# Attention and channel mix on one core: weight loads on 128 partitions, 64-row transposes joined with the k-v sums, two batches mixed out of PSUM, a new order

## The chip, the cores and the metric

The kernel runs on one core of a Trainium2 chip. The metric is the device time of one execution in microseconds (us). One core has five engines that run side by side, each with its own queue of instructions in a fixed order: TensorE (PE, matmuls and transposes), VectorE (DVE), ScalarE (ACT), GpSimd (POOL) and SyncE (SP). SP, ACT and POOL also issue DMAs. Matmul results land in PSUM, 8 banks of 2 KB for each of 128 partitions; everything else lives in SBUF.

## The reference

Linear attention feeds a channel mix in the manner of RWKV. With 8 batches, 8 heads, 576 positions, head width 64, 512 channels and 1024 hidden channels:

```python
q_s = softmax(q, over the 64 channels);  k_s = softmax(k, over the 576 positions)
kv = einsum('bhsd,bhse->bhde', k_s, v)
x  = einsum('bhsd,bhde->bhse', q_s, kv)          # then (batch, position, head*64 + e)
x_prev = x shifted by one position, zeros ahead
xk = mu_k * x + (1 - mu_k) * x_prev
xr = mu_r * x + (1 - mu_r) * x_prev
k = maximum(xk @ w_k, 0);  v = k * k @ w_v;  r = sigmoid(xr @ w_r)
out = r * v
```

The kernel leaves the subtraction of the maximum out, computes in bf16 with float32 sums, and writes the sigmoid by way of tanh.

## The kernel before, in words

**Attention** works on groups: batch b and g = 0 or 1, four heads each, two of them (u = 0, 1) side by side in 128 channels and two (hf = 0, 1) above each other in partitions 0 to 63 and 64 to 127. A partition holds nine neighbouring positions (j = 0 to 8), which makes each load one run of 9*64 floats per head. For each group ACT takes the exponentials of q and k (L423) and casts v (L430), DVE sums q's exponentials over the channels (L437), inverts (L440) and scales (L445), PE transposes the scaled q, nine times 128x128 (L472), and ACT copies the result out (L476). PE sums k-v in 18 matmuls of 64 rows, the two row halves alternating (L453); a column of ones beside v gives k's sum, whose reciprocal (L460, L464) scales the k-v matrix into a weight (L560). PE's X (L566) is then x, transposed: channels on partitions, positions in the order (position in 9, run).

**Mixing.** With that order the previous position is the column 64 to the left, and the first 64 columns come from the end ("edge"). For batches 1 to 7, ACT copies X out (L571) and DVE does edge (L575), difference (L579), scaling by mu (L584) and addition (L589), into xk and xr. For batch 0 the mixing is done on PE: the k-v matrix is multiplied by masks that hold mu and 1-mu (L513, masks built by POOL on L350 and L351), five matmuls (L525) add both terms in PSUM, and one copy each (L530) brings xk and xr out. xk and xr are rings of four batches.

**Main work** runs in units of 512 columns of the ring (and one of 256 per half): k tiles (L646, four matmuls each) with relu on ACT (L631) and square on DVE (L635); then per 128 columns an r tile (L677) with tanh on ACT (L682), a v tile in two halves (L687), the product on DVE (L693) and two stores issued by SP (L703).

**The order** of every engine is written out ahead by a planner (class Plan). An operation has an engine, a length, a due time (`key`), the operations that it depends on and the buffers that it takes and gives back. Due times of the main work come from a clock that starts at MAIN and goes on by PACE times each length; due times of earlier steps are counted back from those that use them, less a lead (`early`, from AHEAD: 1, 4 and 8 us for batch 0, batch 1 and the rest). The planner then plays the engines forward and takes for each the operation that is ready first, by due time among those ready. Loads are issued by ACT, SP and POOL in the order FIRST for batch 0 and by POOL for the rest, behind the weights, in the order of their keys, of which SOON changes a few. POOL's weights wait for the seventh load of batch 0 (GATE). PSUM has four single banks `mm` for main work and two pairs of banks `att`; batch 0's k-v sums use `mm` (pool "early").

Of the kernel before, what the change touches and what calls it, by code (L numbers as in the profile page):

```python
# [15 lines left out]

START = 0.7
HOP = 0.05
LATE = 1e6
SPARE = 0  # L20
LOOK = {"PE": 0.03, "ACT": 0.2, "DVE": 0.1, "POOL": 0.03, "SP": 0.03}
AHEAD = (1.0, 4, 8)
MAIN = 17.0
PACE = 1.148
DMA_RATE = 365.0
DMA_LEAD = 2.5
DMA_TAIL = 0.6

PARTS = {1: [slice(0, 2)], 2: [slice(0, 1), slice(1, 2)]}
FIRST = ((0, 0, ("ACT", "ACT")), (1, 0, ("SP", "SP")), (0, 1, ("ACT", "SP")),  # L30
         (0, 2, ("SP", "SP")), (1, 1, ("SP", "SP")), (1, 2, ("SP", "SP")))
ORDER = (0, 1, 2)
SOON = {(1, 0, 0): 2.2, (1, 0, 1): 2.4, (1, 1, 0): 2.7, (1, 0, 2): 3.5}
GATE = 6
FILL = 0
ON_PE = (0,)
CASTS = (("ACT", "ACT"), ("ACT", "ACT"))
EVAC = ((("ACT", "DVE"), ("ACT", "ACT")), (("ACT", "DVE"), ("ACT", "ACT")))
# [3 lines left out]

# [7 lines left out]
class Op:  # L50


    def __init__(self, engine, occ, lat, key, emit, deps, takes, gives, size):
        self.engine, self.occ, self.lat, self.key = engine, occ, lat, key
        self.emit, self.deps, self.takes, self.size = emit, list(deps), list(takes), size
        self.start = self.end = None
        self.early = 0.0
        for slot in gives:
            slot.last.append(self)


class Plan:

    def __init__(self, pools, shared):
        self.pools = {name: [shared.get((name, i), [(name, i)]) for i in range(n)]
                      for name, n in pools.items()}  # L70
        self.user = {}
        self.ops = []

    def add(self, engine, occ, lat, key, emit, deps=(), takes=(), gives=(), size=0.0):
        op = Op(engine, occ, lat, key, emit, [d for d in deps if d is not None], takes, gives,
                size)
        self.ops.append(op)
        return op

    def slot_time(self, slot):  # L80
        best = None
        for i, parts in enumerate(self.pools[slot.pool]):
            free = 0.0
            for user in (self.user.get(part) for part in parts):
                if user is not None:
                    late = [o.end for o in user.last]
                    free = None if not late or None in late or free is None else max(
                        [free] + late)
            if free is not None and (best is None or free < best[0]):
                best = (free, i)  # L90
        return best
# [9 lines left out]
    def set_due(self):  # L101
        after = {}
        for op in self.ops:
            for d in op.deps:
                after.setdefault(d, []).append(op)
        seen = set()
        for root in self.ops:
            stack = [(root, False)]
            while stack:
                op, closed = stack.pop()  # L110
                if closed and not op.size:
                    for o in after.get(op, ()):
                        op.key = min(op.key, o.key - op.lat - HOP - SPARE)
                    op.key -= op.early
                elif op not in seen:
                    seen.add(op)
                    stack.append((op, True))
                    stack += [(o, False) for o in after.get(op, ())]

    def order(self):  # L120
        self.set_due()
        free = {}
        self.pe_busy = []
        dma_free = 0.0
        waiting = {}
        for op in self.ops:
            waiting.setdefault(op.engine, []).append(op)
        done = []
        left = len(self.ops)
        while left:  # L130
            chosen = None
            for engine, ops in waiting.items():
                now = free.get(engine, START)
                ready = None
                for op in ops:
                    if any(d.end is None for d in op.deps):
                        continue
                    t = max([now] + [d.end + HOP for d in op.deps])
                    ok = True
                    for slot in op.takes:  # L140
                        got = self.slot_time(slot)
                        if got is None:
                            ok = False
                            break
                        t = max(t, got[0] + HOP)
                    if not ok:
                        continue
                    rank = (max(t, now + LOOK[engine]), op.key)
                    if ready is None or rank < ready[0]:
                        ready = (rank, t, op)  # L150
# [4 lines left out]
            for slot in op.takes:  # L155
                slot.index = self.slot_time(slot)[1]
# [8 lines left out]
            elif op.size:  # L165
                dma_free = max(dma_free, t + DMA_LEAD) + op.size / DMA_RATE
# [4 lines left out]
            waiting[op.engine].remove(op)  # L171
            done.append(op)
            left -= 1
        return sorted(done, key=lambda o: o.start)


@with_exitstack
def kernel(
# [13 lines left out]

    B, H, S, D = q.shape
    C = H * D
    F = moe_w_k.shape[1]
    assert S == 576 and D == 64 and H == 8, f"{q.shape=}"
    J = S // 64
    CT = C // 128
    FT = F // 128
    RING = 4 * S  # L200
    UNITS = ((0, 512), (512, 512), (1024, 512), (1536, 512), (2048, 256))
    assert B % 4 == 0

    pools = {"raw": 12, "eq": 3, "ek": 2, "vv": 2, "stat": 4, "qs": 2, "qt": 3, "w": 3, "wp": 4,
             "rz": 3, "xb": 2, "xd": 2, "xm": 3, "k2": 2, "rel": 3, "th": 2, "ot": 3, "mm": 4,
             "att": 2, "early": 2}
    shared = {("early", i): [("mm", 2 * i), ("mm", 2 * i + 1)] for i in range(2)}
    plan = Plan(pools, shared)
# [5 lines left out]
    def buffers(name, shape, dtype, space=None):  # L214
        return [(space or const).tile(shape, dtype, name=f"{name}_{'abcdefghijklmnop'[i]}")
                for i in range(pools[name])]

    raws = buffers("raw", [128, 2, J * D], F32)
    eqs = buffers("eq", [128, J, 2, D], BF16)
    eks = buffers("ek", [128, J, 2, D], BF16)  # L220
    vvs = buffers("vv", [128, J, 130], BF16)
    rsums = [const.tile([128, 2 * J], F32, name=f"rsum_{x}") for x in "abcd"]
    rrecs = [const.tile([128, 2 * J], F32, name=f"rrec_{x}") for x in "abcd"]
    qss = buffers("qs", [128, J, 128], BF16)
    qts = buffers("qt", [128, J, 128], BF16)
    ws = buffers("w", [128, 2, 128], BF16)
    wps = buffers("wp", [128, 2, 2, 128], BF16)
    rzs = buffers("rz", [128, 2], F32)
    xbs = buffers("xb", [128, 2, 64 + S], BF16)
    xds = buffers("xd", [128, 2, S], BF16)  # L230
    xms = buffers("xm", [128, 2, S], BF16)
    k2s = buffers("k2", [128, FT, 512], BF16)
    rels = buffers("rel", [128, 512], BF16)
# [66 lines left out]
    def emit_identity():  # L300
        make_identity(nc, ident[:])
# [468 lines left out]
```

## Time and profile before

| | us |
|---|---|
| median of three runs | 212.07 |
| lowest, highest | 210.74, 212.23 |
| profiled execution, first to last instruction (its span; its own total is not given) | 210.3 |
| PE busy | 192.2 (91%) |
| DVE busy | 160.3 (76%) |
| ACT busy | 150.9 (72%) |
| POOL busy | 43.2 (21%) |
| mean DMA rate over the span | 193 GB/s |

Slices of the page are a fortieth of the span, and a digit is the busy share in tenths. Rows of the chain give start, length and what ran; rows of the timeline give start, length, engine, line, operation, output and inputs, count, and in brackets the idle time ahead and what ended it. A matmul's own row is longer than its share, since matmuls overlap; the chain shows the share. Times are counted from the span's start.

### The profile page before, as it was taken

What the parts mean: (1) busy time and instruction counts of PE and PEld (TensorE: products, weight loads), DVE (VectorE), ACT (ScalarE), POOL (GpSimd) and SP (SyncE); (2) the same over time, 40 slices, a digit from 0 to 9 for tenths busy, and PEclk for the clock granted to TensorE, in tenths of its full rate; (3) what the DMA queues carried; (4) which work ended last, traced back from release to release, by engine and by line L of the source; (5) the groups of instructions that cost most, each with busy time, mean ns of one, the idle gap of its engine ahead of it and who ended that gap; (6) DMA issues with size and microseconds to landing.
All of it is one profiled execution on the core that took longest, in us unless ns stands there. A gap on an engine that the chain in (4) does not pass through costs nothing.

```text
span 210.3 us, 3597 instructions
## 1 busy us (share of the span) xinstructions
PE 192.2 (91%) x1283; PEld 97.2 (46%) x1283; DVE 160.3 (76%) x364; ACT 150.9 (72%) x229; POOL 43.2 (21%) x72
## 2 busy tenths in 40 slices
PE   3089998967999999999999999999999999999991
PEld 0065444433544544445467444445444554444740
DVE  6488684999999999999959995957796469632531
ACT  5596798998999999759599977338964862452440
POOL 3793656534334132301100000000000000000000
PEclk9999999999999999999999999999999999999999
DMA  6999999999999999983871130350034003502424
GB/s 216 367 215 201 346 267 394 392 405 403 392 395 404 404 383 339 317 277 112 245 196 41 31 69 0 71 119 14 6 86 111 2 3 85 115 0 50 102 51 100
DMA packets 15898, 40.62 MB, mean 193 GB/s; under 512 B 2300, under 2 KB 3848, under 8 KB 15880
## 3 DMA queue, kind: packets, MB, share of 16 engines
q0 software_dynamic: 8384, 27.40, 39.7%
q1 hardware_dynamic: 7064, 12.10, 20.4%
q10 hardware_dynamic: 432, 0.88, 1.3%
q8 instruction: 10, 0.16, 0.3%
q14 instruction: 8, 0.07, 0.1%
HBM read 33.56 MB, written 9.44 MB: 204 GB/s over the span
## 4 chain that ended last, share of the span: by engine, by line
PE 82%; DVE 7%; ACT 4%; DMA 3%; issue 1%; ACTq 0%; DVEq 0%
PE mm_b L646 9%; PE mm_c L646 8%; PE mm_a L687 7%; PE mm_d L687 7%; PE mm_b L687 7%; PE mm_a L646 6%; PE mm_c L687 6%; PE mm_d L677 5%; PE mm_d L646 5%; PE mm_c L677 4%; DMA raw_b<-in_k_dram 3%; PE mm_a L677 2%; PE att_a L472 2%; PE att_a L453 2%; PE att_b L453 2%; PE att_b L472 2%
## 5 line engine op out<-in xcount | busy, mean ns | idle before, releaser
L646 PEld LDWEIGHTS <-wk_bf 128*128 128x128 bf16 x320 | 30.4, 98 | 31.0 <-issue 2.3
L646 PE MATMUL mm_b<-xk,wk_bf 128*128 128x512 bf16 (+1 forms) x96 | 23.2, 357 | 0.0
L646 PE MATMUL mm_c<-xk,wk_bf 128*128 128x512 bf16 (+1 forms) x92 | 22.6, 361 | 0.0
L677 PEld LDWEIGHTS <-xr 128*128 128x128 bf16 x144 | 13.4, 98 | 16.0 <-issue 0.7
L687 PEld LDWEIGHTS <-k_a 128*128 128x128 bf16 x144 | 13.5, 98 | 15.8 <-issue 0.5
L687 PEld LDWEIGHTS <-k_b 128*128 128x128 bf16 x144 | 13.4, 98 | 15.7
L646 PE MATMUL mm_a<-xk,wk_bf 128*128 128x512 bf16 (+1 forms) x72 | 17.1, 355 | 0.0
L646 PE MATMUL mm_d<-xk,wk_bf 128*128 128x512 bf16 (+1 forms) x60 | 14.9, 358 | 1.6 <-DVE xk L589 1.6
L677 PE MATMUL mm_d<-wr_bf,xr 128*128 128x512 bf16 x56 | 14.4, 379 | 0.0
L687 PE MATMUL mm_a<-wv_bf,k_a 128*128 128x512 bf16 x48 | 12.3, 379 | 0.0
L682 ACT ACTIVATE th_a<-mm_d 128x512 f32<-128x512 f32 x12 | 7.2, 602 | 6.8 <-PE mm_d L677 6.6
L677 PE MATMUL mm_c<-wr_bf,xr 128*128 128x512 bf16 x40 | 10.3, 379 | 0.1
L687 PE MATMUL mm_d<-wv_bf,k_a 128*128 128x512 bf16 x40 | 10.3, 379 | 0.0
L687 PE MATMUL mm_c<-wv_bf,k_b 128*128 128x512 bf16 x40 | 10.3, 379 | 0.0
L687 PE MATMUL mm_b<-wv_bf,k_b 128*128 128x512 bf16 x40 | 10.1, 379 | 0.0
L472 PEld LDWEIGHTS <-qs_a 128*128 128x128 bf16 x72 | 4.9, 103 | 8.6 <-DVE qs_a L445 7.4
L635 DVE TENSOR_TENSOR k_a<-rel_a 128x512 bf16<-128x512 bf16 (+1 forms) x13 | 5.1, 391 | 4.6 <-ACT rel_a L631 4.5
L631 ACT ACTIVATE rel_a<-mm_b 128x512 bf16<-128x512 f32 (+1 forms) x10 | 5.4, 539 | 4.0 <-PE mm_b L646 3.8
L687 PE MATMUL mm_a<-wv_bf,k_b 128*128 128x512 bf16 x32 | 8.2, 379 | 0.0
L687 PE MATMUL mm_d<-wv_bf,k_b 128*128 128x512 bf16 x32 | 8.2, 379 | 0.0
L687 PE MATMUL mm_c<-wv_bf,k_a 128*128 128x512 bf16 x32 | 8.2, 379 | 0.0
L682 ACT ACTIVATE th_b<-mm_a 128x512 f32<-128x512 f32 x6 | 3.6, 594 | 6.3 <-PE mm_a L677 6.3
(258 smaller groups left out, 452.5 us busy)
## 6 DMA issues: line engine op xcount, KB each, us to landing
out_dram<-ot_a SPq DMA_DIRECT2D x24, 128.0 KB, 2.7
out_dram<-ot_b SPq DMA_DIRECT2D x24, 128.0 KB, 2.4
out_dram<-ot_c SPq DMA_DIRECT2D x24, 128.0 KB, 2.7
raw_a<-in_q_dram POOLq DMA_DIRECT2D x3, 576.0 KB, 10.3
raw_c<-in_k_dram POOLq DMA_DIRECT2D x2, 576.0 KB, 10.3
raw_b<-in_v_dram POOLq DMA_DIRECT2D x2, 576.0 KB, 10.5
raw_d<-in_q_dram POOLq DMA_DIRECT2D x2, 576.0 KB, 10.2
raw_e<-in_k_dram POOLq DMA_DIRECT2D x2, 576.0 KB, 10.9
```

The source lines that it names most:

```text
L453: nc.tensor.matmul(kv_of(kvp, hf)[:, 0:129], lhsT=eks[ek.index][r, j, :, :].rearrange("p u d -> p (u d)"), rhs=vvs[vv.index][r, j, 0:129], ...
L472: nc.tensor.transpose(out=transposed()[:, j, :], in_=qss[qs.index][:, j, :], identity=ident[:])
L631: nc.scalar.activation(out=rels[rel.index][:, 0:n], in_=bank(kf)[:, 0:n], func=ACT.Relu, scale=HALF_ROOT)
L635: nc.vector.tensor_tensor(out=k2s[k2.index][:, fc, 0:n], in0=rels[rel.index][:, 0:n], in1=rels[rel.index][:, 0:n], op=ALU.mult)
L646: nc.tensor.matmul(bank(kf)[:, 0:n], lhsT=wk_bf[:, ct, fc * 128:(fc + 1) * 128], rhs=xs[0][:, ct, c0:c0 + n], start=(ct == 0), stop=(ct == ...
L677: nc.tensor.matmul(bank(rps), lhsT=xs[1][:, ct, c:c + 128], rhs=wr_bf[:, ct, :], start=(ct == 0), stop=(ct == CT - 1))
L682: nc.scalar.activation(out=ths[th.index][:], in_=bank(rps), func=ACT.Tanh, scale=0.5)
L687: nc.tensor.matmul(bank(vps), lhsT=k2s[k2.index][:, ft, 128 * m:128 * m + 128], rhs=wv_bf[:, ft, :], start=(ft == 0), stop=(ft == FT - 1))
```

## The change

- **Weights.** w_k and w_r were loaded to partitions 0 to 63 and 64 to 127 by two DMAs each; now one DMA writes 128 partitions, with row 2e+u on a partition where it was 64u+e. w_k is split by columns (two tiles of 512) instead of by channel tiles. The k-v weight `w` is written with the same interleaving (last index u), so that X comes out in that order, and mu is turned to it by a copy ahead of its transpose.
- **Transposes.** Nine of 128x128 become 18 of 64 rows by 128 columns, one half into each bank of a pair. For batches 2 to 7 they and the 18 k-v matmuls are one block on PE that takes both `att` buffers; for batches 0 and 1 (SPLIT) they stay separate.
- **Mixing.** Batches 0 and 1 (FUSED): X into PSUM as for the others; for each of xk and xr and each hf, ACT copies X out scaled by 1-mu, DVE copies the edge, and one DVE operation takes mu times X from PSUM plus the shifted copy. Masks, their loads and their operations are gone. Batches 2 to 7 keep the earlier mixing.
- **Order.** New constants; a lead for each batch and group; due times aren't counted back through main operations; three passes, each with main operations due when the last pass started them; FIRST has k of group 0 ahead of q of group 1; of batch 1 to 7 one load (q of batch 2, group 0) goes ahead of w_v and all of batch 1; only units 0 and 1 split their k tiles by channel halves, for their first four tiles; tanh is due earlier.
- **Buffers and tail.** Three instead of two of ek, vv and qs; five output tiles for three. The very last tile's v is computed in two halves of 256 columns, each stored by SP and ACT.

```diff
-AHEAD = (1.0, 4, 8)
-MAIN = 17.0
-PACE = 1.148
+MAIN = 17.837
+PACE = 1.101
-FIRST = ((0, 0, ("ACT", "ACT")), (1, 0, ("SP", "SP")), (0, 1, ("ACT", "SP")),
-         (0, 2, ("SP", "SP")), (1, 1, ("SP", "SP")), (1, 2, ("SP", "SP")))
-SOON = {(1, 0, 0): 2.2, (1, 0, 1): 2.4, (1, 1, 0): 2.7, (1, 0, 2): 3.5}
-ON_PE = (0,)
+FUSED = (0, 1)
+SPLIT = (0, 1)
+EARLY_UNITS = 2
+AHEAD = {(0, 0): 4.01, (0, 1): 1.59, (1, 0): 6.36, (1, 1): 1.67, (2, 0): 13.33, (2, 1): 9.59,
+        (3, 0): 9.47, (3, 1): 9.29, (4, 0): 7.84, (4, 1): 8.09, (5, 0): 3.2, (5, 1): 7.98, (6,
+        0): 2.31, (6, 1): 12.19, (7, 0): 5.85, (7, 1): 5.11}
+FIRST = ((0, 0, ("ACT", "SP")), (0, 1, ("ACT", "SP")), (1, 0, ("SP", "SP")), (0, 2, ("SP",
+        "SP")), (1, 1, ("SP", "SP")), (1, 2, ("ACT", "SP")))
+SOON = {(2, 0, 0): 2.63}
+PASSES = 3
...
-    def weight_part(dst, src, n, u, c0, c1):
-        ap = bass.AP(tensor=src.tensor, offset=src.offset + (4 * u + c0) * D * n,
-                     ap=[[n, 64], [D * n, c1 - c0], [1, n]])
-        return nc.gpsimd.dma_start(out=dst[64 * u:64 * u + 64, c0:c1, :], in_=ap)
+    def weight(dst, src, n, col, width, gated=False):
+        ap = bass.AP(tensor=src.tensor, offset=src.offset + col,
+                     ap=[[n, D], [4 * D * n, 2], [D * n, CT], [1, width]])
+        ld = kn.nc.gpsimd.dma_start(out=dst[:], in_=ap)
...
-    mask_zeros = plan.add("DVE", 1.8, 1.9, 0, emit_mask_zeros)
-    rows_load = plan.add("SP", 0.9, 0.9, -600, emit_mu_rows_load, size=10.0)
-    rows_done = plan.add("PE", 0.86, 0.98, -501, emit_mu_rows, [rows_load, consts], [rows_slot])
-    wide = plan.add("ACT", 0.48, 0.6, 0, emit_mu_wide, [rows_done], [], [rows_slot])
-    mu_masked = [plan.add("POOL", 1.55, 1.6, -2 + m, lambda m=m: emit_mu_mask(m),
-                          [wide, mask_zeros]) for m in range(2)]
+    mu_turn = add("DVE", 0.2, 0.28, LATE, emit_mu_turn, [mu_load])
+    mu_done = add("DVE", 0.16, 0.26, LATE, emit_mu_copy, [mu_t], gives=[mu_slot])
+    mu_done.early = 6.0
...
         def transpose_q():
             for j in range(J):
-                nc.tensor.transpose(out=transposed()[:, j, :], in_=qss[qs.index][:, j, :],
-                                    identity=ident[:])
+                for hf in range(2):
+                    r = slice(64 * hf, 64 * hf + 64)
+                    kn.nc.tensor.transpose(out=turned(hf)[:, j, :],
+                                           in_=kn.qss[qs.index][r, j, :],
+                                           identity=kn.ident[r, r])
...
+        if split:
+            tr = add("PE", 0.5, 0.67, step, transpose_q, scaled + [identity], [qtp], [qs],
+                     name=f"T{tag}")
+            kvm = add("PE", 0.73, 0.8, step, kv, expk + castv, [kvp], [ek, vv], name=f"KV{tag}")
+        else:
+            def block():
+                transpose_q()
+                kv()
+            tr = kvm = add("PE", 1.1, 1.2, step, block, scaled + [identity] + expk + castv,
+                           [qtp, kvp], [qs, ek, vv], name=f"TKV{tag}")
...
+        if b in FUSED:
...
+                    def rest(xe=xe, hf=hf, c=c):
+                        kn.nc.scalar.activation(out=kn.xes[xe.index][:, hf, 64:64 + S],
+                                                in_=flat(xp[hf])[:, 0:S], func=ACT.Copy,
+                                                scale=kn.rest[:, c:c + 1])
+                    def edge(xe=xe, hf=hf):
+                        t = kn.xes[xe.index]
+                        kn.nc.vector.tensor_copy(out=t[:, hf, 1:64], in_=t[:, hf, 576:639])
+                    def fuse(xe=xe, hf=hf, c=c, m=m):
+                        kn.nc.vector.scalar_tensor_tensor(
+                            out=kn.xs[m][:, 2 * g + hf, c0:c0 + S], in0=flat(xp[hf])[:, 0:S],
+                            scalar=kn.mu[:, c:c + 1], in1=kn.xes[xe.index][:, hf, 0:S],
+                            op0=ALU.mult, op1=ALU.add)
...
+            parts = [slice(0, 256), slice(256, 512)] if last and m == tiles - 1 else [slice(0, C)]
...
+                        q = kn.nc.scalar if len(parts) == 2 and i == 1 else kn.nc.sync
+                        q.dma_start(out=dst, in_=kn.ots[ot.index][64 * i:64 * i + 64, part])
...
+def ordered(plan):
+    for _ in range(PASSES):
+        made = plan.order()
+        for op in plan.mains:
+            op.key = op.start
+    return made
```

## The prediction

> **What bounds the kernel now.** I read the page's slices first, then busy time in windows of 10 us, the chain that ended last, the timeline of 15 to 50 us and the rows of single tiles. The slices, each 5.26 us:
>
> ```profile
> PE   3089998967999999999999999999999999999991
> DVE  6488684999999999999959995957796469632531
> ACT  5596798998999999759599977338964862452440
> DMA  6999999999999999983871130350034003502424
> ```
>
> TensorE (PE) is full from the tenth slice to the last but one. The windows (after the stretch and its length: PE, weight loads, DVE, ACT, POOL, clock, DMA share, GB/s) say how full:
>
> ```profile
> 30.00:40.00 10.00, 9.27 (x72) 4.60 (x70) 6.60 (x16) 9.34 (x16) 6.47 (x9) 1.00 1.08 367
> 40.00:50.00 10.00, 7.02 (x71) 3.65 (x70) 9.86 (x20) 8.78 (x11) 4.21 (x6) 1.00 1.04 405
> 50.00:60.00 10.00, 10.00 (x71) 4.97 (x70) 9.85 (x23) 9.90 (x16) 3.86 (x7) 1.00 1.04 393
> ```
>
> PE loses 3 us in 40:50 and almost nothing after. So three stretches can move the end: until the first main matmul, the stall for batch 1, and the tail; from 50 us on only PE work counts. The chain gives PE's prices:
>
> ```profile
> 47.77 0.68 DVE xk L589
> 48.48 0.59 PE mm_d L646 x2
> ...
> 68.69 0.50 PE att_b L472 x9
> 69.20 0.86 PE mm_c L646 x4
> ...
> 73.15 0.63 PE att_b L453 x18
> 73.78 0.97 PE mm_c L646 x4
> ...
> 203.88 1.74 PE mm_b L687 x8
> 205.62 0.04 DVEq L693
> 205.65 0.04 issue
> 205.70 0.69 DVE ot_c L693
> ```
>
> Four full matmuls take 0.864 us, 0.216 each. The page counts 320 of L646 (64 of them half wide), 144 of L677, 288 of L687: 720 full ones, 155.5 us. Nine transposes cost 0.50; the 18 k-v matmuls 0.63, and the four matmuls behind them 0.97 instead of 0.86, so 0.74 in all. With X (two halves of 0.245 in the chain) an attention group takes 0.50+0.74+0.49 = 1.73 us of PE. The timeline shows where PE's useful work starts and what stops it:
>
> ```profile
> 18.82 0.60 PE L646 MATMUL mm_c<-xk,wk_bf 128*128 128x512 bf16 x2
> ...
> 45.34 0.70 PE L453 MATMUL att_b<-vv_a,ek_a 64*128 64x129 bf16 x18 [1.21 <-ACT vv_a L430]
> ...
> 48.48 0.59 PE L646 MATMUL mm_d<-xk,wk_bf 128*128 128x512 bf16 x2 [1.62 <-DVE xk L589]
> ```
>
> From 18.8 to 205.6 are 186.8 us. Work in it: 155.5, 14 groups of batches 1 to 7 at 1.73 (24.2), and some 1.7 of batch 0's mixing. **So 5.4 us are lost, nearly all before 48.5.** Behind 205.6 come 4.7 us: eviction and the last stores.
>
> **The profiled run's own time** is given only as its span, 210.3. The three runs have a median of 212.07 and a lowest of 210.74, so 0.4 to 1.9 us lie around a span. I add 1.8, which ties the sum to the median.
>
> **Part by part.**
>
> *Batch 0 mixed out of PSUM.* Gone are eight mixings of five matmuls (0.49 each at full clock, 3.9 us), the DVE clearing of the mask (1.76), ACT's wide copy (0.58), eight POOL operations (about 3.5, off the path: the gate on weights opens at 10.09, the mask is done at 9.83), two small loads ahead of SP's first data load (it is issued at 1.45; 0.7 earlier now) and 16 DVE weight products (0.34). Added: four X (0.245), per group four ACT evictions with a scale (nearest row 0.64, plain), four edge copies (0.13 to 0.24 for two heads) and four DVE mixes from PSUM (nearest row 0.76, the eviction on L530). The scaled copy may cost up to 0.1 more than the plain one, or nothing; the mix lies between 0.69 (L693, 512 columns from PSUM) and 0.86. Start of main work: k-v of group 0 ends at 13.5 now; 0.5 less for the earlier loads; reciprocals 0.3, weights 0.8, two X at half clock 1.0, two evictions 1.1, edge and two mixes with overlap 1.3: 17.5. Other DVE work in the queue may sit between; I take 17.8, bounds 16.8 and 19.5, one microsecond before 18.82. Of mixing work some 0.3 us is left behind this start, against 1.7.
>
> The clock: nine transposes take 1.14 us at 11.09 and 0.67 later, and the k-v pairs at 15.72 are already quick. PE gets less to do ahead of 17.8; if it is still at half clock there, about 3.4 us of main work at half pace would cost 1.7. The range has room for that.
>
> *Batch 1 the same way.* Per group, ACT gives up two evictions (0.53 apart) and gets four: plus 1.1 to 1.4 us. DVE gives up difference, four scalings and two mixes (some 3.7) and gets four mixes and edges (some 3.3). The chain from X to the first mix is shorter: eviction, edge, mix (1.6) against two evictions, edge, difference, two scalings, mix (3.3).
>
> *Loads.* DMA is busy without a break in 8 to 50 us (share 1.0 to 1.2), also while weights go to 64 partitions at a time. So I take nothing for 128 partitions. Weights come at 164 to 199 GB/s in written bytes between 12 and 20 us, twice that read, and plain loads later at 390 to 415: should the weights reach that, 5.2 MB land 1.5 us sooner; nearer to the rows of weights is zero. The order matters more. Now the last load of batch 1 is issued at 27.6 and lands 9.1 us later, 36.7. In the new order q of batch 2 (0.59 MB, 1.6 us at 365 GB/s) and all of w_v stand ahead of batch 1: its first group lands some 2 us later than now, its last at about 37.5 to 38. POOL's five weight issues for eight save queue time only; it waits there for landings.
>
> *The stall.* With v of the last group at 37.7: cast 1.2, k-v 0.8, reciprocal and weights 0.8, X 0.4, eviction, edge, mix 2.1 for two halves: xk whole at 43.0, against 48.44 now. Until then PE has 17.3 us of unit 0 (80 full matmuls) + 0.3 + 3.5 (two groups) + 1.7 (half of four k tiles of unit 1) from 17.8: 40.6. **The stall is 2.4 us; with 0.7 between the halves of unit 0 and 0.5 elsewhere, 3.6 lost against 5.4.** ACT is the cover that could fail: from 30 us on it has 12 to 13 us of such work for these 13. Where DVE takes batch 2's sum and scaling first, as now (43.09 to 46.1), 2.6 more are late. Bounds 1 and 7.
>
> *64-row transposes in a block.* Eighteen for nine, each moving 64 columns. The k-v matmuls show that two row halves run side by side: 18 in 0.63, 0.062 a pair with 129 columns. A pair with 64 columns needs between half of that (0.031, if the columns set it) and all (0.062, if the loads do): 0.28 to 0.56 us for 0.50. I take 0.35, nearer to the columns' end, since the loads of 64 rows are issued faster than the pairs (18 in 0.52 at 45.34). A block costs 0.35+0.74 = 1.09 for 1.24. Twelve blocks: 1.8 us less, bounds 3 less and 1 more. Batch 1's separate transposes get the change of row mode of their own (0.11 and more): zero. The block takes both big PSUM buffers at once and waits for both evictions; what is queued behind it on PE is main work. With one group each 13 us and five of occupancy, it is hidden if the order places it late enough.
>
> The Trainium skill, "TensorE: Matmul & The Clock Gate", section "LDWEIGHTS (loading the stationary operand)", speaks against this: a load costs by its columns, the rows don't count, so 18 loads of 128 columns would cost as much as 18 full ones. No estimate here rests on it; by it the transposes take the last rival's time.
>
> *Steady stage, buffers, orders.* X reads a contiguous operand at the same 512+64 columns: zero. Third buffers and five output buffers: zero, PE waits for neither after 50 us. DVE and ACT are over 97% busy from 50 to 80 us, then 50 to 95%: batch 7's last xk mix starts at 174.8 and its unit at 178.6, and DVE idles some 20 us between 100 and 170, so both carry a PE that is 6 us ahead.
>
> *Tail.* The last tile's second half is evicted in about 0.35 instead of 0.69 and its two stores go out on two queues instead of one after the other (issue 1.11 for both): 0.8 less, 3.9.
>
> **Sum:** 17.8 + 155.5 + 0.3 + 24.2 - 1.8 + 3.6 + 3.9 = 203.5; with 1.8 around it **205.3 us**.
>
> **Rivals.**
> 1. *Forecast*, 205.3: chance 0.52.
> 2. *The stall nearly goes* (1 us left: weights at the loads' rate), pairs at 0.031, start 16.8: 200.3 + little; I say 202. For it: DMA sustains 400 later; against: ACT has no gap left. 0.18.
> 3. *The stall stays, 6.5 us,* since ACT's added evictions stand ahead of batch 1's casts: 208.2. For it: cast vv_b starts at 38.68, 2 us after its data. 0.13.
> 4. *Order too tight later:* batches 5 and 6 get leads of 2.3 and 3.2 us where all had 8; five waits of one us behind PE's fixed order: 210.3. Against: nothing waits now after 50. 0.08.
> 5. *Slower:* the transposes don't pair. At 0.0556 each, the pace of the rows now, 18 take 1.0: 0.65 over my figure, in 14 groups 9.1 us: 214.4. It decides from 0.52 us per group, a pair at 0.097. The k-v rows, 0.062 a pair with as many loads, speak against. 0.09. By the Trainium skill's page on TensorE, section on LDWEIGHTS, it would come out so.
>
> About 1% is what a measurement here can tell from no change. Cases 1 to 3 are faster by over 1% (below 209.95), less 0.02 for their edges: 0.81; same 0.09 (case 4 and an edge), slower 0.10. The range goes from the sum of the lower bounds, 200.3, to just past case 4, 211.0; outside are case 5 and edges.
>
> **What would show it.** The first k matmul near 17.8; the wait for batch 1's xk (now ending at 48.48) ended near 43; a block of 36 in about 1.1 us, its transposes' pairs 0.03 to 0.06 apart; PE without gaps from then on; the last main matmul near 199.6, then 3.9 us. It is wrong if pairs run singly, if ACT's evictions push the wait beyond 46, or if PE waits for xk or xr after 60 us.

## The result, and the profile after

The changed kernel takes 214.43 us (median of four runs, 214.11 to 214.79), the kernel before 212.15 on the same chip: a ratio of 1.0116, with an interval of 1.0072 to 1.0161. It is slower by about 1.2%, where 3% less was forecast, and lies outside the range of 200.3 to 211.0. Executions over 1.5% above the fastest of their kernel are left out of the times and ratios of this document. The profiled execution took 214.79, its span is 213.0 us, so 1.8 us lie around it, as the sum had assumed.

The slices of the changed kernel's page (5.3 us each):

```profile
PE   0165798974999999999999999999999999999992
DVE  1957698988999999999559996999849439942432
ACT  3795869999999999968389997868654664362350
PEclk9999999996699999999999999999999999999999
DMA  6999999999999999699633040233024204212423
```

PE is again full from the eleventh slice on. All that is new stands ahead of it: the third to sixth slice (6, 5, 7, 9, against 8, 9, 9, 9 before), the tenth (4, against 7), and a clock of 0.6 in the tenth and eleventh. The windows of 10 us (after the stretch: PE, weight loads, DVE, ACT, POOL, clock, DMA share, GB/s):

```profile
20.00:30.00 10.00, 8.17 (x33) 3.25 (x32) 8.29 (x17) 6.82 (x11) 2.15 (x4) 1.00 1.16 296
30.00:40.00 10.00, 9.07 (x75) 4.19 (x74) 8.86 (x21) 9.19 (x17) 7.93 (x12) 1.00 1.03 392
40.00:50.00 10.00, 7.40 (x65) 3.51 (x64) 8.61 (x18) 9.66 (x14) 4.34 (x6) 0.99 1.04 408
50.00:60.00 10.00, 8.39 (x59) 3.38 (x59) 9.34 (x22) 9.28 (x14) 2.89 (x4) 0.67 1.03 397
```

The timeline's last matmuls end at 208.97, as those of the kernel before did at 205.6; the first of two half products has begun by then:

```profile
208.37 0.60 PE L621 MATMUL mm_b<-wv_b,k_b 128*128 128x256 bf16 x4
208.63 0.42 DVE L627 SCALAR_TENSOR_TENSOR ot_a<-th_b,mm_c 128x256 f32<-128x256 f32 x1 [0.62 <-PE mm_c L621]
```

From the first main matmul (18.24) to 208.97 are 190.7 us. The work in it is 155.5 + 24.2 + 0.3, as forecast, less 2.9 for the blocks (below): 177.1. **So 13.6 us are lost, against 5.4 before and 3.6 forecast**: some 4.7 until 26.9, 5.8 from there to 51.46, 2.8 until 56.9, and 0.3 in all the rest.

*The first loss, batch 0.* The timeline of 17 to 22 us (start, length, engine, line; in brackets the idle time ahead and what ended it):

```profile
17.37 0.82 DVE L471 SCALAR_TENSOR_TENSOR xk<-att_a,mu,xe_a 128x576 bf16<-128x576 f32 x1
...
18.22 0.74 ACT L462 ACTIVATE xe_b<-att_a,rest 128x576 bf16<-128x576 f32 x1 [0.56 <-DVE xk L471]
...
18.38 0.82 DVE L471 SCALAR_TENSOR_TENSOR xk<-att_b,mu,xe_a 128x576 bf16<-128x576 f32 x1
...
19.23 0.74 ACT L462 ACTIVATE xe_b<-att_b,rest 128x576 bf16<-128x576 f32 x1 [0.27 <-DVE xk L471]
...
20.82 0.81 DVE L471 SCALAR_TENSOR_TENSOR xr<-att_b,mu,xe_b 128x576 bf16<-128x576 f32 x1
20.95 0.64 PE L410 MATMUL att_a<-qt_b,w_b 128*128 128x512 bf16 x2 [0.27 <-DVE xr L471]
...
21.63 0.74 ACT L462 ACTIVATE xe_c<-att_a,rest 128x576 bf16<-128x576 f32 x1 [1.66 <-DVE xr L471]
```

ACT's second scaled copy of a pair (for xr) reads the same PSUM pair as DVE's first mix (for xk), and starts only when that mix has ended: 0.56 and 0.27 us of waiting. The two engines read one pair by turns, so a pair is held by four operations one behind the other, from X at 15.6 until the mix that starts at 20.09 has ended (20.9). PE can't put X of the second group there before 20.95, and ACT, which copies that X, idles for 1.66 us. Not all of this is the turns: in DVE's order the edge copy of the other half stands ahead of the mix at 20.09, and DVE idles 0.72 us for its operand. And some 1.6 of the 4.7 us are no waits at all: PE's first matmuls run at half pace (see the half clock below).

*The second loss, batch 1.* The timeline of 38 to 53 us:

```profile
38.92 0.41 PE L410 MATMUL att_b<-qt_c,w_c 128*128 128x512 bf16 x2
...
41.89 1.30 ACT L339 CAST vv_a<-raw_a 128x576 bf16<-128x576 f32 x2
...
45.36 0.44 PE L366 MATMUL att_a<-ident,qs_b 64*128 64x64 bf16 x18 [0.36 <-DVE xr L471]
...
46.90 0.70 PE L378 MATMUL att_b<-vv_a,ek_a 64*128 64x129 bf16 x18 [0.35 <-DVE xr L471]
...
51.33 0.81 DVE L471 SCALAR_TENSOR_TENSOR xk<-att_b,mu,xe_c 128x576 bf16<-128x576 f32 x1
51.46 1.31 PE L569 MATMUL mm_c<-xk,wk_a 128*128 128x512 bf16 x2 [2.28 <-DVE xk L471]
52.57 1.06 PE L569 MATMUL mm_d<-xk,wk_a 128*128 128x512 bf16 x2
```

The second group's v is cast at 41.9 to 43.2, but its transposes and sums start at 45.36 and 46.90: both pairs are still held by the first group's mixing, of which X was at 38.7. Of the 7.9 us for which the second pair is held (38.92 to 46.85), its four readings take 3.2. In the rest ACT takes k's exponentials, a tanh and the casts of v first, and DVE takes products and q's scaling: that is the written order, not the turns. The second half of unit 1 starts at 51.46, where 43.0 was forecast. The third loss follows it: the next k matmuls are 0.85 us a pair apart, half pace, at a clock of 0.67 in that window.

### The profile page after: what moved, and what is told of

Its sections match the earlier page's. It is cut to its first block, busy times and chain, and to the rows that moved or that the text cites. A ratio compares the mean times of both kernels' runs of the same rounds, so it can differ in the third digit from the quotient of the medians.

```text
span 213.0 us, 3840 instructions
## 1 busy us (share of the span) xinstructions
PE 188.0 (88%) x1401; PEld 92.4 (43%) x1401; DVE 163.3 (77%) x376; ACT 155.1 (73%) x234; POOL 38.3 (18%) x61
## 4 chain that ended last, share of the span: by engine, by line
PE 70%; DVE 12%; ACT 10%; DMA 3%; issue 2%; SPq 0%; DVEq 0%; ACTq 0%
PE mm_c L569 7%; PE mm_d L621 7%; PE mm_b L621 6%; PE mm_d L569 6%; PE mm_a L569 6%; PE mm_c L621 6%; PE mm_a L621 6%; PE mm_b L569 6%; PE mm_b L601 4%; PE mm_a L601 3%; DMA raw_b<-in_q_dram 3%; PE mm_d L601 3%; PE mm_c L601 3%; DVE xk L471 3%; DVE xr L471 2%; PE att_b L378 2%
## 5 line engine op out<-in xcount | busy, mean ns | idle before, releaser
L569 PEld LDWEIGHTS <-wk_a 128*128 128x128 bf16 x160 | 15.9, 101 | 23.9 <-issue 9.4
L569 PEld LDWEIGHTS <-wk_b 128*128 128x128 bf16 x160 | 15.3, 99 | 16.8 <-issue 2.0
L569 PE MATMUL mm_c<-xk,wk_a 128*128 128x512 bf16 (+1 forms) x52 | 13.3, 362 | 5.2 <-DVE xk L471 5.0
L569 PE MATMUL mm_c<-xk,wk_b 128*128 128x512 bf16 (+1 forms) x40 | 10.2, 380 | 0.6 <-ACT rel_a L554 0.6
L569 PE MATMUL mm_d<-xk,wk_a 128*128 128x512 bf16 (+1 forms) x40 | 10.7, 383 | 0.0
L569 PE MATMUL mm_a<-xk,wk_a 128*128 128x512 bf16 (+1 forms) x40 | 10.4, 376 | 0.0
L601 PE MATMUL mm_b<-wr,xr 128*128 128x512 bf16 x40 | 10.3, 379 | 0.0
L569 PE MATMUL mm_d<-xk,wk_b 128*128 128x512 bf16 (+1 forms) x40 | 9.4, 358 | 0.0
L569 PE MATMUL mm_b<-xk,wk_b 128*128 128x512 bf16 (+1 forms) x40 | 9.4, 358 | 0.0
L569 PE MATMUL mm_a<-xk,wk_b 128*128 128x512 bf16 (+1 forms) x40 | 9.4, 358 | 0.0
```

What stands on the lines that cost most here:

```text
L569: kn.nc.tensor.matmul(kn.bank(kf)[:, 0:n], lhsT=kn.wk[fc // 4][:, ct, (fc % 4) * 128:(fc % 4) * 128 + 128], rhs=kn.xs[0][:, ct, c0:c0 + n] ...
L601: kn.nc.tensor.matmul(kn.bank(rps), lhsT=kn.xs[1][:, ct, c:c + 128], rhs=kn.wr[:, ct, :], start=(ct == 0), stop=(ct == CT - 1))
```

## The experiments

All times are medians, each with its ratio to the kernel before on the same chip. "Last product" is where the first product of the last v tile starts on DVE (205.7 before, 208.6 after). Where that tile is split, in all kernels but the one before, e7, e11 and e12, another 0.34 us of matmuls lie behind it.

**1. The mixing out of PSUM, batch 1 or both batches without it.**

```diff
-FUSED = (0, 1)
+FUSED = (0,)        # e1
+FUSED = ()          # e2
```

> The changed kernel with batch 1 mixed as before (X copied out twice by ACT, then edge, difference, scaling, addition from SBUF); batch 0 stays mixed out of PSUM. Theory A (ACT's evictions and DVE's mixes read the same PSUM pair in turns and hold both pairs for 8 us in batch 1): the pairs are free 1.6 us after X, xk of batch 1 is whole near 47 instead of 52, PE's clock does not fall behind it, time 209 to 210.5. Rival B (batch 1's loads come too late in the new order): loads are as in the changed kernel, so 213.5 to 214.5.

Measured: 216.83 us, 1.021 (1.0147 to 1.0274), last product 210.2, above both forecasts.

> The changed kernel with no batch mixed out of PSUM. A: batch 0's second group is no longer held up by the first, though its first half starts some 1.5 us later; main work runs without gaps from 22 on; 208 to 210.5, near the run with batch 0 fused. Rival B: 213 to 214.5. If batch 0's mixing out of PSUM is worth what the forecast gave it (start 1 us sooner), this run is 1 us slower than the one with batch 1 alone unfused.

Measured: 215.30 us, 1.0158 (1.0079 to 1.0237), last product 208.5, above the forecasts too. Without the mixing out of PSUM the waits at batch 0 go, since a pair is free after one plain copy; the second group's X waits for that copy alone and the first main matmul is 1.7 us later (e2's timeline of 16 to 20 us):

```profile
16.90 0.64 PE L410 MATMUL att_a<-qt_b,w_b 128*128 128x512 bf16 x2 [0.25 <-ACT xb_a L489]
17.44 0.64 PE L410 MATMUL att_b<-qt_b,w_b 128*128 128x512 bf16 x2
...
19.94 1.01 PE L569 MATMUL mm_c<-xk,wk_a 128*128 128x512 bf16 x2 [1.86 <-DVE xk L507]
```

The first k pairs of e2 run at half pace as well, and yet it is 0.9 us ahead where the second half of w_k comes in (25.96, against 26.89). But unit 1's second half still starts at 52.2 (e1) and 50.8 (e2), and 1.8 and 1.6 us are newly lost between 120 and 125 us (PE 8.0 and 8.2 of 10 from 120 to 130). In e2 the pairs are not what holds the second group: its sums run at 41.84 and its X at 45.39, but then DVE takes the sum and the scaling of batch 2's q (45.80 and 47.98, 2.7 us together) ahead of batch 1's xk. My theory, that the mixing of batch 1 is the cause of the stall, missed: taking it out is not enough.

**2. The loads of batch 1 in their old places.**

```diff
-SOON = {(2, 0, 0): 2.63}
+SOON = {(1, 0, 0): 2.2, (1, 0, 1): 2.4, (1, 1, 0): 2.7, (1, 0, 2): 3.5}
```

> The changed kernel with the earlier order of POOL's loads (three loads of batch 1 ahead of the first half of w_v, its first v between the halves, q of batch 2 behind). B: batch 1's second group lands 1.6 us sooner, its first group 5 us sooner, the wait for xk ends 3 us sooner, 211 to 212.5. A: the pairs are still held in turns, 213 to 214.5.

Measured: 218.74 us, 1.0314 (1.0252 to 1.0376), last product 212.3, above both forecasts. The operands of the second group are ready earlier (v cast by 39.7, not 43.2), and it helps nothing, for the pairs are held; DVE scales a later batch's q (42.99, 1.36 us) ahead of the first group's last two mixes. Its timeline of 38 to 53 us:

```profile
38.96 0.78 ACT L339 CAST vv_a<-raw_l 128x576 bf16<-128x576 f32 x1
...
45.81 0.44 PE L366 MATMUL att_a<-ident,qs_a 64*128 64x64 bf16 x18 [0.22 <-DVE xr L471]
...
52.68 0.58 PE L569 MATMUL mm_b<-xk,wk_a 128*128 128x512 bf16 x1 [2.97 <-DVE xk L471]
```

**3. The planner is told of the turns.** ACT's second copy depends on DVE's first mix of the same half.

```diff
+            turn = [None, None]
-                    o = add("ACT", 0.62, 0.74, step, rest, [made[hf], mu_done, late_consts],
+                    o = add("ACT", 0.62, 0.74, step, rest, [made[hf], mu_done, late_consts, turn[hf]],
+                    turn[hf] = o          # behind the DVE mix
```

> The changed kernel whose order counts on the turns: each second eviction from a PSUM bank is planned behind the first mix from it. The waits on the chip are the same, only what is placed between them differs. If it is the order's blindness that costs, 211.5 to 213; if it is the time for which the pairs are held (A), 213.5 to 214.5.

Measured: 215.69 us, 1.0171 (1.0099 to 1.0244), last product 210.4, above both forecasts. With the change's leads the knowledge alone brings nothing; unit 1 starts its second half at 49.7, and there is a wait of 1.84 us at 123.

**4. The half clock.**

```diff
...
+        if op.name in ("KV11", "X111"):
+            for i in range(4 if op.name == "KV11" else 8):
+                nc.tensor.matmul(kn.bank(held[i % 4]), lhsT=kn.zeros[:],
+                                 rhs=kn.xs[0][:, 0, 512:1024], start=False, stop=False)
```

> The changed kernel with 12 matmuls by a tile of zeros, added into the banks of unit 1's half-done k sums, so that the result stays the same: 4 behind the k-v sums of batch 1's second group (46.9 us), 8 behind its x (48.5 us). Orders, leads and every other instruction stay. Theory A (the 16 k matmuls from 51.46 us ran at half clock because TensorE had idled most of the 5 us before): at 0.216 us each the fillers take 2.6 us of the gap, the clock stays at 1.0 in 50 to 60 us, and 2.5 to 2.8 us go: 211.6 to 212.2 us. Rival B (the clock fell for another reason, so that the fillers run slow too, 0.43 us each, or delay the x matmuls): 214 to 216 us and a clock of 0.6 to 0.8 in that window.

Measured: 214.44 us, 1.0095 (1.0066 to 1.0123), last product 208.2. The clock did what theory A says and the time did not. First a window of this kernel, then its timeline of 53 to 56 us:

```profile
50.00:60.00 10.00, 8.25 (x70) 3.71 (x68) 9.65 (x24) 10.00 (x15) 2.90 (x4) 1.00 1.04 397
```

```profile
53.67 1.03 PE L571 MATMUL mm_c<-xk,wk_b 128*128 128x512 bf16 x4
54.67 0.44 PE L368 MATMUL att_a<-ident,qs_c 64*128 64x64 bf16 x18
55.95 0.70 PE L380 MATMUL att_b<-vv_b,ek_b 64*128 64x129 bf16 x18 [0.84 <-DVE xr L473]
```

The k matmuls from 51.44 on run at full pace (in the changed kernel 12 of them are slow, not the 16 that I had expected), and batch 2's block starts at 54.67 instead of 56.86. Then its sums wait for a pair that batch 1's mixing holds (1.0 us of the 2.2 gone), and 0.2 to 0.25 us more go at 65 and at 80 us; 0.4 is left at the end. So the slow clock that follows the gap costs next to nothing at the end. What the timeline shows in its place are waits for ACT, DVE and the two pairs.

**5. The joined 64-row blocks alone**, in the kernel before.

```diff
-                nc.tensor.transpose(out=transposed()[:, j, :], in_=qss[qs.index][:, j, :], identity=ident[:])
+                for hf in range(2):
+                    r = slice(64 * hf, 64 * hf + 64)
+                    nc.tensor.transpose(out=turned(hf)[:, j, :], in_=qss[qs.index][r, j, :], identity=ident[r, r])
...
+            tr = kvm = plan.add("PE", 1.0, 1.17, pe_key, block,
+                                scaled + [identity] + expk + castv, [qtp, kvp], [qs, ek, vv])
```

> The kernel before with one part of the change alone: q is turned in 64-row halves (18 transposes instead of 9) and, from batch 2 on, in one block with the k-v sums; weights, mixing, loads and leads stay as they were. Theory A (the blocks are the part of the change that pays: 1.00 us a group in the changed kernel's trace against 1.24 before, and TensorE has no spare time after the first 50 us): 12 groups by 0.24 us, 2.9 us less, about 209.3 us, between 208.3 and 210.5, with the block again near 1.0 us. Rival B (the time saved comes back as waits, since VectorE and ScalarE are busy over 9.8 of 10 us between 40 and 70 us and the joint block takes both PSUM pairs at once): 211.5 to 213.

Measured: 215.61 us, 1.0132 (1.0071 to 1.0193), last product 209.4. Rival B, and beyond it: main work starts 1.0 us sooner (17.82) and each block is shorter, but other losses eat more. The stall at 46 to 49 costs 3.1 us of waits, about as before (3.0), but behind it ten k matmuls run at half pace (48.90 to 53.12, some 2 us more); 1.05 are lost at 20 to 21 for w_k's load and 2.8 between 92 and 98, where DVE and ACT run late. (From 40 to 70 us only VectorE had been over 9.8 of 10 us busy before; ScalarE had 8.8 to 9.9.) A part that saves work made the kernel slower under an order that was made for other work.

**6. The same instructions under another order.** That left the order. The planner's end was a usable guide: for e1 to e4 it lay within 0.7 us of the chip's last product (for the changed kernel itself it was 2.2 too early). So the 16 leads and the places of the loads of batches 1 and 2 were searched with it, for the change with the turns known (e9) and for the change with nothing mixed out of PSUM (e10).

```diff
-SOON = {(2, 0, 0): 2.63}
+SOON = {(1, 0, 0): 0.55, (1, 0, 2): 0.28, (1, 1, 0): 1.12, (1, 0, 1): 1.38, (1, 1, 1): 2.04, (1, 1, 2): 0.79,
+        (2, 1, 2): 4.23, (2, 1, 1): 4.53, (2, 0, 1): 4.39}                    # e10
-AHEAD = {(0, 0): 4.01, (0, 1): 1.59, (1, 0): 6.36, (1, 1): 1.67, (2, 0): 13.33, ...
+AHEAD = {(0, 0): 2.57, (0, 1): 9.6, (1, 0): 10.58, (1, 1): 10.0, (2, 0): 9.21, ...     # e10
```

> The changed kernel with all its instructions, both batches mixed out of PSUM, in another order: the planner is told that ScalarE's second reading of a PSUM pair comes after VectorE's first (as in the run where the order knows the turns), and the 16 leads and the loads' places of batches 1 and 2 were searched again with that plan. The plan's end of the last main matmul was 209.7, 209.2, 212.6 and 210.0 us for the four variants so far, and 210.2, 208.5, 212.3 and 210.4 us on the chip, within 0.7; for the changed kernel, whose plan lets the two engines read at once, 206.4 against 208.6. It is 200.3 us here. Theory A (the time went into an order that was made for a plan without the turns): last main matmul at 200 to 202.5 us, stall of unit 1 under 2 us in all, no half clock, 206 to 209 us in all. Rival B (ScalarE and VectorE, over 9 of 10 us busy from 30 to 100 us, set the end whatever the order): 212 to 215 us.

Measured: 208.80 us, 0.9802 (0.9743 to 0.9861), last product 202.2.

> The changed kernel with no batch mixed out of PSUM (all eight are copied to SBUF and mixed there, as batches 1 to 7 before), with leads and load places searched for this; the plan's last main matmul is at 199.2 us. Theory A (orders): last main matmul at 199 to 202 us, 205 to 208.5 us in all, level with or up to 1.5 us below the run with the mixing out of PSUM and searched leads, so that the mixing out of PSUM is not what the gain needs. Rival B (the two engines' work sets the end): 212 to 216 us, as the run with no mixing out of PSUM under the change's leads (215.3). Rival C (the mixing out of PSUM is worth its turns once the order fits): 2 us or more above the other run of this pair.

Measured: **205.88 us, 0.9665 (0.9614 to 0.9717)**, last product 199.6. The times are those of theory A for both, and rival B falls; that e10 lies 2.9 us below e9 is more than the 1.5 expected. e10 beats both kernels, by 3.3% and, by the ratios, 4.5%. Its windows:

```profile
20.00:30.00 10.00, 10.00 (x70) 4.23 (x69) 10.00 (x24) 8.10 (x15) 4.90 (x8) 1.00 1.15 294
30.00:40.00 10.00, 9.55 (x78) 4.50 (x77) 8.88 (x24) 7.61 (x13) 4.61 (x7) 1.00 1.13 327
40.00:50.00 10.00, 10.00 (x54) 4.39 (x54) 9.75 (x19) 9.42 (x14) 3.78 (x6) 1.00 1.03 399
50.00:60.00 10.00, 10.00 (x112) 5.06 (x109) 9.90 (x21) 10.00 (x14) 4.46 (x7) 1.00 1.04 401
```

Over these 40 us PE is busy for 39.6 us, against 33.0 in the changed kernel, while DVE does more (38.5 against 35.1) and ACT as much (35.1 against 35.0). So their time was not short; it went to other work first. e9, which has the changed kernel's own instructions, shows that the order does it. It is 2.9 us behind e10; PE's waits before 25 us (1.79, 0.45, 0.15 and 0.82, all for xk) are part of that, but with one searched order each, the price of the mixing out of PSUM as such is not shown.

**7. What the search brings without the change's instructions, and without knowledge of the turns.** e11 is the kernel before with searched leads and load places, e12 the same with the blocks, e13 the changed kernel searched with its own plan.

> The kernel before with every instruction as it was, and 16 leads and load places of batch 1 searched in the same way as for the two runs that were faster; its plan's last main matmul goes from 203.5 to 202.3 us (the plan prices a group's transposes and sums under what they take, so its own kernel's 205.6 us stood at 203.5). Theory A (the gain of those two runs needs the change's instructions, the joined blocks above all): 1.1 us less by the plan, 209.5 to 212.5 us. Rival B (a searched order alone brings it, whatever the instructions): 205 to 208 us.

Measured: 210.06 us, 0.9892 (0.9839 to 0.9946), last product 203.6.

> The kernel before with 64-row transposes and joined blocks (slower than before by 1.3% under the old leads), with leads and load places searched for it; the plan's last main matmul goes from 204.6 to 201.2 us. Theory A (the blocks save 2.9 us of TensorE's work, and the old leads gave it back in waits): 3 us or more under the run with the old leads, 206.5 to 211 us, and below the kernel before. Rival B (the joined blocks bring waits that no order takes away): 212.5 to 216 us.

Measured: 210.78 us, 0.9890 (0.9847 to 0.9933), last product 205.3.

> The changed kernel with both batches mixed out of PSUM and leads and load places searched as long again, but with the plan that lets ScalarE and VectorE read one PSUM pair at once; its last main matmul is planned at 201.1 us, that of the plan which knows the turns was at 200.3 and came out at 202.2. Theory A (the plan's ignorance of the turns costs the 2.2 us by which it missed the changed kernel): 211 to 213 us, last main matmul 2 to 4 us behind its plan. Rival B (the turns matter little, the search was what counted): 208.5 to 210 us, last main matmul within 1.9 us of its plan.

Measured: 211.16 us, 0.9930 (0.9902 to 0.9958), last product 205.0, 3.9 us behind its plan (e9: 1.9). So theory A each time: an order alone is worth about 1% to the old instructions; the blocks' order takes back 4.8 us from e7; and in e13 a plan that lets both engines read one pair at once misses by 2 us more than e9's, which doesn't. That is one searched order of each kind: e1 and e3 had such plans too and came within 0.5 us of them. e12 is only level with e11, although PE is busy for 187.8 us instead of 190.4: 3.0 us between 46 and 51 are lost to waits for qs and xk, as in e7. Why no order was found there that keeps the saving stays open.

**8. The wide transposes under e10's order**, every operation in its place. The copy out and X's operand go back to the earlier layout too; X keeps its pace (0.24 a half).

```diff
-            for hf in range(2):
-                kn.nc.tensor.transpose(out=turned(hf)[:, j, :], in_=kn.qss[qs.index][r, j, :], identity=kn.ident[r, r])
+            kn.nc.tensor.transpose(out=turned()[:, j, :], in_=kn.qss[qs.index][:, j, :], identity=kn.ident[:])
...
```

> The fastest kernel so far (no batch mixed out of PSUM, searched leads, 205.88 us), every operation in the same place of every engine's order, with q turned 128 rows at a time again (9 transposes instead of 18, as in the kernel before), inside the same blocks. Theory A (the 64-row halves run in pairs and cost 0.25 to 0.28 us a group where nine wide ones cost about 0.5, and TensorE has no idle time left to hide it): 16 groups by 0.24 us, 3.0 to 4.0 us more, 208.9 to 209.9 us. Rival B (ScalarE and VectorE bound the kernel there, so that TensorE's longer blocks fill its waits): under 1 us more, 205.5 to 206.9 us.

Measured: 208.59 us, 0.9817 (0.9751 to 0.9882), last product 202.2: 2.6 us behind e10. A block with its neighbours, first in this kernel, then in the changed one:

```profile
63.13 0.67 PE L365 MATMUL att_a<-ident,qs_a 128*128 128x128 bf16 x9
63.73 0.70 PE L375 MATMUL att_b<-vv_a,ek_a 64*128 64x129 bf16 x18
64.36 1.04 PE L600 MATMUL mm_a<-wr,xr 128*128 128x512 bf16 x4
```

```profile
62.58 1.03 PE L601 MATMUL mm_a<-wr,xr 128*128 128x512 bf16 x4
63.53 0.44 PE L366 MATMUL att_a<-ident,qs_a 64*128 64x64 bf16 x18
63.81 0.69 PE L378 MATMUL att_b<-vv_c,ek_c 64*128 64x129 bf16 x18
64.43 1.04 PE L621 MATMUL mm_d<-wv_b,k_b 128*128 128x512 bf16 x4
```

From start to start the transposes take 0.60 wide (with the change of row mode behind them) and 0.28 as halves, where the change of mode, 0.09, comes ahead (62.58 to 63.53 is 0.95 for 0.86). A block is 1.23 or 0.99: 0.24 for each of the 12 joined ones make 2.9, just over the 2.6 found. Theory A's size for 16 groups was too high. Where unit 1 comes to the second half of w_k, e14 is only 0.4 behind (46.72 against 46.34), so the four groups of batches 0 and 1 cost 0.4 in all and the 12 blocks 2.2.

**9. Which part of the order.** e10's instructions with its load places and the change's leads (e15), or its leads and the change's load places (e16).

> No batch mixed out of PSUM; the load places are those of the fastest kernel (all of batch 1 among the first weights, ahead of w_v), the leads those of the change. Theory A (the late loads of batch 1 are the cause): most of the 9.4 us between the two orders comes from here, as the plan has it (last main matmul 202.6 us, against 209.2 with both as in the change and 199.2 with both searched): 208 to 211 us, and unit 1's second half starts before 48 us. Rival B (the leads put later batches' work ahead on ScalarE and VectorE, whenever the loads land): 212.5 to 216 us, second half of unit 1 at 50 us or later.

Measured: 209.84 us, 0.9886 (0.9841 to 0.9930), last product 203.8.

> The same instructions with the searched leads and the change's load places (four loads of batch 1 behind w_v). Theory A (the loads): the stall of unit 1 stays; planned last main matmul 206.9 us, 212 to 215 us in all, and second half of unit 1 at 49 us or later. Rival B (the leads): 206 to 210 us.

Measured: 214.28 us, 1.0081 (1.0049 to 1.0114), last product 209.5. Theory A both times. The second half of unit 1, first in e15, then in e16:

```profile
46.06 0.59 PE L571 MATMUL mm_a<-xk,wk_a 128*128 128x512 bf16 x2 [1.02 <-DVE xk L509]
```

```profile
51.94 0.61 PE L572 MATMUL mm_b<-xk,wk_a 128*128 128x512 bf16 x2 [2.17 <-DVE xk L510]
```

Of the 9.4 us between e2 and e10 the loads' places alone bring 5.5, the leads alone 1.0 (by the ratios 2.7% and 0.8% of 4.9%; the 0.8% is not clear of the two intervals); the rest needs both.

**Together**, with the change's leads, the stall has two causes, and either one alone keeps it:

| | batch 1's loads behind w_v | batch 1's loads early |
|---|---|---|
| batches 0 and 1 mixed out of PSUM | 214.4, second half at 51.5 | 218.7, at 52.7 |
| nothing mixed out of PSUM | 215.3, at 50.8 | 209.8, at 46.1 |

The early places are those of the kernel before in the upper row and searched ones in the lower, so the entries of the right column are not the same loads to the last one. Other places for loads also change the order that the planner writes for every engine, so it is not shown how much of a step to the right is the landing and how much the order behind it.

## Why the prediction was wrong

By its own terms, forecast and measured, in us of span:

| term | forecast | measured |
|---|---|---|
| first main matmul | 17.8 | 18.24 |
| matmuls, groups, rest of batch 0 | 180.0 | 180.0 (the same counts and prices) |
| blocks | -1.8 | -2.9 |
| lost | 3.6 | 13.6 |
| tail | 3.9 | 4.0 |
| sum | 203.5 | 213.0 |

- **The failed step is "xk whole at 43.0", and with it the 3.6 us lost**, outside its own bounds of 1 and 7. The sign named for it, a wait beyond 46, came: 51.46. The landing was right (v of the last group, issued at 32.65, landed 5.5 us later, at 38.1; 37.7 was taken), but everything behind it was added up as if nothing stood ahead. The cast ended at 43.2 instead of 38.9, since ACT took q and k of the same group, two tanh and the first group's two scaled copies in between (+4.3). The sums started at 46.90, since the pairs were held until 46.85 (+3.7). From the sums to xk whole (52.1) took 5.2 instead of 4.1. I had named ACT as "the cover that could fail" and gave it a rival at 208.2; e2 and e16 show that with late loads the stall stays even when ACT has no scaled copies. The prediction's remark on DVE taking batch 2's sum and scaling first ("2.6 more are late") was priced and left out of the sum; e2 shows just that. The holding of the pairs I had not in the sum at all.
- **The edge and mix "with overlap" for batch 0** was the same mistake in small, and the "0.7 between the halves of unit 0" went with it: 4.7 us were lost there. I priced ACT's second copy and DVE's first mix as work side by side; they take turns. The Trainium skill, "PSUM — Partial Sum Buffer", section "PSUM bank collisions raise a hardware error", says that accesses of two engines to the same bank and partitions have to be kept apart, reads against reads too. The trace agrees: ACT waits 0.56 and 0.27 us for DVE's reading to end. I had not weighed it.
- The durations came out at the upper end: scaled copy 0.74 (0.64 to 0.74 forecast), up to 0.81 in batch 1, mix 0.82 (0.69 to 0.86).
- **The blocks** were right in kind and undersized: the pairs run side by side, 0.28 us for 18 (0.35 taken), and a block takes 0.99 to 1.00 (1.09). e14 confirms it on the time: 2.6 us. The last rival, that pairs run singly, fell; that its time, 214.4, is the one measured is chance. I had let the Trainium skill's "TensorE: Matmul & The Clock Gate", section "LDWEIGHTS (loading the stationary operand)", speak for it. The price that it gives, by columns and not by rows, the trace bears out: a load of 64 rows takes 95 ns, one of 128 rows 98. What failed was my step from the price to the time, since the loads of the two row halves overlap: 18 loads and 18 matmuls in 0.28 us are 0.016 each.
- **The half clock at the start** did come: the pair of k matmuls at 19.63 takes 1.06 and X at 20.95 0.64, where later ones take 0.59 and 0.42. It lies inside the first loss, some 1.6 us of it.
- **The order later.** Rival 4 named leads that are too tight for batches 5 and 6. In the changed kernel PE waits 0.15 us there (122.2); but e1 to e4 wait 1.6 to 1.9 us each between 120 and 127. The leads fit one configuration.
- **Loads, buffers, the steady stage** cost what was said: nothing can be seen of 128-partition weight loads in PE's waits.
- **Tail:** right: 4.0 us from the last matmul's end, where 3.9 was forecast and 4.7 was before. The two half products take 0.42 each, 0.38 apart, and the last four stores are issued on two queues within 1.4 us.
- **Two slips in the working:** the last rival's "0.52 us per group" gives 212.6 with its 14 groups, while 1% slower, 214.2, takes 0.64; and the lower bounds named (start 1.0, stall 2.6, blocks 1.2 less) add up to 200.5, not 200.3. Neither touches the sum.

The sum as such is reachable: e10's span is 204.0 us, against 203.5 forecast. Against the kernel before it has 0.65 us later main work, 2.9 less for the blocks, 1.7 less of batch 0's matmuls, 1.8 less lost, and 0.6 less tail: 6.3 us, the difference of the spans (210.3 to 204.0; the last matmuls of e10 end at 199.9).

## What to carry to other kernels

When a chain behind a landing is added up, put into the sum what stands ahead in each engine's queue and who holds the buffers at that time; the rows before and the change's code give both. A PSUM buffer that two engines read by turns is held at least for the sum of their readings (3.2 us in batch 1) and for whatever the order puts between them (4.7 more), so a single plain copy out of it can be the faster mixing even with more operations behind. An order that was fitted to one set of instructions is part of them: judge a change of instructions only under an order fitted to it, or a saving of work (e7) reads as a loss.

## What the runs showed that I had not expected

- A gap that costs a slow clock need not cost time: the 12 k matmuls that ran at half pace from 51.46 to 56.86 came back to full pace in e8, and the median stayed at 214.4.
- The window's clock does not show every slow stretch. In e10 the clock of 20 to 30 us reads 1.00, while its first pairs run at half pace, 0.85 us from start to start, and later ones at 0.43 (timeline of 20 to 25 us):

```profile
20.28 1.06 PE L572 MATMUL mm_c<-xk,wk_a 128*128 128x512 bf16 x2
21.13 1.06 PE L572 MATMUL mm_a<-xk,wk_a 128*128 128x512 bf16 x2
...
23.66 0.59 PE L572 MATMUL mm_c<-xk,wk_a 128*128 128x512 bf16 x2
24.09 0.59 PE L572 MATMUL mm_a<-xk,wk_a 128*128 128x512 bf16 x2
```

  From 19.47 to 23.66 these are 4.2 us; in e14 the like stretch, 19.87 to some 22.7, is 2.8. The Trainium skill, "TensorE: Matmul & The Clock Gate", Part 1, has half pace after an idle window and some 3.4 us of work to end it, which lies between. In the kernel before PE was at full pace in time: it worked nearly without a break from 11.09, and its first k pairs are 0.43 apart at 18.82.
